# Two more buffers for rows of x in the last stage, loaded further ahead

## The chip, the cores and the metric

The kernel runs on one core of one Trainium2 chip. The metric is device time in microseconds (us). The kernel before took 1497.77 us (median of 3 runs, 1496.35 to 1498.45) when the work began.

Engine names in the profile: PE is TensorE's matmuls, PEld its weight loads, DVE VectorE, ACT ScalarE, POOL GpSimd, SP the engine that issues most loads. A "q" after a name (SPq) is that engine's instruction queue. "L1389" is line 1389 of the kernel.

## The reference, cut to what matters

The kernel computes the output of one block and its gradients. The block is a layer norm with modulation, a spectral filter, a second layer norm and a gated MLP. x has 2048 rows of 576 in bf16; the kernel holds them as 16 tiles of 128 x 576, each called "a row" below.

```python
h = _layernorm(x, axis=-1) * (1 + ca) + sa
x = x + ga * _A_ref(h, A_w_r, A_w_i)          # rfft2 * W, irfft2
h = _layernorm(x, axis=-1) * (1 + cb) + sb
x = x + gb * _B_ref(h, w_gate, w_up, w_down)  # the output, and B's gradients
_out, _vjp = jax.vjp(f, A_x, A_w_r, A_w_i, B_w_gate, B_w_up, B_w_down, c, w_mod)
```

The last stage of the kernel finishes the gradient of x: for each row it transforms back, normalises x again, applies the backward formula of the layer norm and stores the row. Two other jobs fill the stage: the rest of the output (`y_piece`, which keeps PE busy through `fill.run`) and the gradient of w_mod (`mod_grad`).

## The kernel before

The places of the buffers in SBUF, the loads, and the row loop (cuts are marked with `...`). `Ring(...).next()` hands out buffers in turn; a load into a reused buffer waits until the last reader of that buffer is done.

```python
with tc.manual_schedule(engines={PE}):       # only PE keeps the order of the text
...
x_r = Ring(span(RA, 3, 1152) + [ACC + 14464], [D])       # four buffers for x
gl_r = Ring(span(RA + 3456, 3, 1152) + [ACC + 15616], [D])
...
def load_xg(j):
    load1(xl, x_r, x_v, j, sp)                           # x row j, on SP's queue
    load1(gl, gl_r, gx1_d, j, sp)
...
for j in range(3):
    load_xg(j)
...
for j in range(18):
    if j < 16:
        if j and j + 2 < 16:
            load_xg(j + 2)
        Hs[j] = stage_bi(j, Gt, e_r, H_r)                # PE; L585 on ACT, L587/L588 on DVE
    ...
    if 1 <= j < 17:
        jj = j - 1
        stage_ai(Hs[jj])
        gh = gh_r.next()
        ac.copy(halves(gh), bank[:, 2:4, 0:288])         # L1387
        n = xl[jj]
        act(n[:], n[:], ACT.Identity, bias=..., scale=...)            # L1389, in place
        ...
        tt(gn[:], gh[:], opc, MUL)                                    # L1393
        tt(q[:], gh[:], n[:], MUL)                                    # L1394
        tt(t2[:], q[:], opc, MUL)                                     # L1395
        act(gn[:], gn[:], ACT.Copy, scale=..., accum_out=s[:, 0:1])   # L1396
        act(t2[:], t2[:], ACT.Copy, scale=..., accum_out=s[:, 1:2])   # L1397
        ts(s[:, 0:1], s[:, 0:1], -1.0 / D, None, MUL)                 # L1398
        act(t2[:], n[:], ACT.Identity, bias=..., scale=...)           # L1399, last reader of x
        tt(gn[:], gn[:], t2[:], ADD)                                  # L1400
        tt(gn[:], gn[:], gl[jj][:], ADD)                              # L1401
        ...
        fill.run(2.2)                                    # y's matmuls L1087, copy out L1090
    fill.run(2.2)
    ...
    while mdone < min(18, 6 * j // 5):
        ...
        mod_grad(*mgs[k], i)                             # L1259 (reads w_mod), L1260
        ...
```

## Time and profile before

The profiled run took 1495.91 us, its span 1494.1 us. The page's busy table and its chain of waits (what ended last, followed back to the start) say that TensorE is the limit of the whole:

```profile
PE 1458.8 (98%) x11108; PEld 968.2 (65%) x11108; DVE 773.3 (52%) x1651; ACT 549.5 (37%) x1048; POOL 347.8 (23%) x510
PE 80%; DMA 6%; DVE 5%; ACT 4%; issue 3%; POOL 1%; SPq 0%; DVEq 0%; ACTq 0%; POOLq 0%
```

So only what makes PE stand still, or slows its clock, in the last stage can cost time there. The PE timeline of the stage (start us, busy us, engine, line, operation; in brackets the idle time before it and what ended that) has four such places between 1376 and 1476 us:

```profile
1395.52 5.14 PE L1087 MATMUL bank<-arena 128*128 128x288 bf16 x27 [1.96 <-ACT arena L1090]
1420.00 0.40 PE L581 MATMUL bank<-arena 128*128 128x288 bf16 x2 [0.78 <-DVE arena L588]
1433.28 0.41 PE L581 MATMUL bank<-arena 128*128 128x288 bf16 x2 [1.23 <-DVE arena L588]
1441.91 3.47 PE L1087 MATMUL bank<-arena 128*128 128x288 bf16 x27 [0.59 <-ACT arena L1090]
```

The first is also followed by a slow spell: 27 matmuls take 5.14 us, against 3.47 us for the same 27 in the last line. The table of stretches shows the clock that was granted meanwhile (stretch, length, PE busy with its instructions, PE clock, DMA share, GB/s):

```profile
1395.00:1397.00 2.00, 1.48 (x12) 0.94 0.54 221
1397.00:1399.00 2.00, 2.00 (x10) 0.50 0.70 191
1399.00:1401.00 2.00, 2.00 (x14) 0.71 0.94 292
```

Why was ACT late? Its timeline just before the first stall:

```profile
1386.34 0.87 ACT L1399 ACTIVATE arena<-arena 128x576 bf16<-128x576 bf16 x1
1387.12 0.38 ACT L585 COPY arena<-bank 128x288 f32<-128x288 f32 x1
1387.40 0.64 ACT L1387 CAST arena<-bank 128x576 bf16<-128x576 f32 x1
1392.80 0.87 ACT L1389 ACTIVATE arena<-arena 128x576 bf16<-128x576 bf16 x1 [4.77 <-DMA arena<-in_A_x_dram]
1393.57 0.76 ACT L1396 ACTIVATE arena<-arena 128x576 bf16<-128x576 bf16 x1
```

And the same moment in the chain, in order of time:

```profile
1386.34 0.87 ACT arena L1399
1387.21 0.03 ACT arena L585
1387.24 5.54 DMA arena<-in_A_x_dram
1392.78 0.03 issue
1392.80 0.87 ACT arena L1389
```

Read these together. The L1399 at 1386.34 is row 0's, the L1387 at 1387.40 is row 1's, and L1396 at 1393.57 is row 1's. The L1389 at 1392.80 is row 4's: four L1389 had already run, the last from 1371.30 us. The load of row 4 could start only when row 0's L1399 had let go of the buffer, it took 5.54 us to land, and ACT stood still for it although row 4 was three rows away. The waits view sums such waits (engine, line, waited for: us in total, times, longest), for 1376 to 1494 us:

```profile
ACT arena L1389 <- DMA arena<-in_A_x_dram: 19.6, 9, 4.8
DVE arena L1259 <- DMA arena<-in_w_mod_dram: 7.6, 4, 2.5
```

The second line is on DVE: `mod_grad` stands in DVE's queue before its w_mod rows have landed, and L588, for which PE waits, stands behind it.

### The profile page before, as it was taken

Reading aid. Unit: us, or ns where it says so; the run is one execution under the profiler, and the core shown is the slowest. Engines: PE = TensorE matmul, PEld = TensorE weight load, DVE = VectorE, ACT = ScalarE, POOL = GpSimd, SP = SyncE. Lnnn points to the kernel's source line nnn. Section 1 sums busy time; section 2 is a strip of 40 time slices with the busy share of each in tenths; the row PEclk is TensorE's granted clock in tenths of the full one; section 3 lists DMA queues with packets and bytes.
Section 4 is the critical chain, followed back from the end, with each engine's and each line's share of the span. In section 5 each row is a group of like instructions: output and inputs, shape, how many; then the busy total and the mean of one; then the engine's idle time right before and its main releaser. Section 6 shows DMA issues by size and latency. Waiting matters only on the chain.

```text
span 1494.1 us, 28278 instructions
## 1 busy us (share of the span) xinstructions
PE 1458.8 (98%) x11108; PEld 968.2 (65%) x11108; DVE 773.3 (52%) x1651; ACT 549.5 (37%) x1048; POOL 347.8 (23%) x510
## 2 busy tenths in 40 slices
PE   8999999999999999999999999999999989999998
PEld 5444443677677677677677677677677666677666
DVE  6533596533543543543543543543543698577665
ACT  6756675212212212212212212212212266334566
POOL 1344322113113113113113113113112013242211
PEclk9999999999999999999999999999999999999999
DMA  9657996968477467568567467567567389667773
GB/s 347 176 150 158 225 242 165 215 132 174 122 130 178 120 128 178 119 130 178 120 129 177 119 130 178 120 130 177 119 124 161 78 225 302 231 212 195 232 240 101
DMA packets 417050, 252.79 MB, mean 169 GB/s; under 512 B 319730, under 2 KB 384692, under 8 KB 416660
## 3 DMA queue, kind: packets, MB, share of 16 engines
q1 hardware_dynamic: 388706, 166.53, 49.5%
q0 software_dynamic: 27440, 83.65, 18.4%
q8 instruction: 87, 1.43, 0.4%
q10 hardware_dynamic: 770, 0.80, 0.2%
q14 instruction: 47, 0.39, 0.1%
HBM read 98.52 MB, written 76.26 MB: 117 GB/s over the span
## 4 chain that ended last, share of the span: by engine, by line
PE 80%; DMA 6%; DVE 5%; ACT 4%; issue 3%; POOL 1%; SPq 0%; DVEq 0%; ACTq 0%; POOLq 0%
PE bank L807 9%; PE bank L809 8%; PE bank L838 8%; PE bank L885 8%; PE bank L889 8%; PE bank L944 5%; PE bank L1087 5%; PE bank L947 5%; PE bank L946 5%; PE bank L945 5%; PE bank L371 3%; PE bank L375 3%; PE bank L802 3%; PE bank L905 2%; DMA arena<-in_w_mod_dram 1%
## 5 line engine op out<-in xcount | busy, mean ns | idle before, releaser
L958 DVE TENSOR_TENSOR arena<-arena,bank 128x576 f32<-128x576 f32 x256 | 193.0, 754 | 307.1 <-PE bank L947 307.1
L813 ACT CAST arena<-bank 128x512 bf16<-128x512 f32 x144 | 84.4, 586 | 385.3 <-PE bank L803 377.0
L947 PE MATMUL bank<-arena 128*128 128x288 bf16 x576 | 164.9, 286 | 0.0
L944 PE MATMUL bank<-arena 128*128 128x288 bf16 x576 | 164.3, 285 | 0.4 <-DVE arena L956 0.2
L946 PE MATMUL bank<-arena 128*128 128x288 bf16 x576 | 164.7, 286 | 0.0
L945 PE MATMUL bank<-arena 128*128 128x288 bf16 x576 | 164.5, 286 | 0.0
L885 PE MATMUL bank<-arena 128*128 128x256 bf16 x1152 | 149.5, 273 | 3.6 <-DVE arena L871 1.8
L1087 PE MATMUL bank<-arena 128*128 128x288 bf16 x1152 | 150.0, 288 | 2.6 <-ACT arena L1090 2.6
L889 PE MATMUL bank<-arena 128*128 128x256 bf16 x1152 | 149.3, 273 | 0.0
L807 PE MATMUL bank<-arena 128*128 128x512 bf16 x576 | 148.7, 381 | 0.0
L809 PE MATMUL bank<-arena 128*128 128x512 bf16 x576 | 147.8, 379 | 0.0
L1087 PEld LDWEIGHTS <-arena 128*128 128x128 bf16 x1152 | 112.1, 98 | 34.7 <-issue 5.8
L838 PE MATMUL bank<-arena 128*128 128x288 bf16 x1024 | 128.1, 286 | 0.0
L885 PEld LDWEIGHTS <-arena 128*128 128x128 bf16 x1152 | 110.8, 98 | 20.6 <-issue 7.1
L889 PEld LDWEIGHTS <-arena 128*128 128x128 bf16 x1152 | 112.3, 98 | 13.7
L838 PEld LDWEIGHTS <-arena 128*128 128x128 bf16 x1024 | 100.2, 98 | 28.2
L817 DVE TENSOR_TENSOR arena<-arena 128x512 bf16<-128x512 bf16 x144 | 61.1, 424 | 105.6 <-ACT arena L813 101.6
L735 POOL DMA_DIRECT2D arena<-ghh_d x36 | 20.0, 556 | 395.2 <-DVE arena L816 386.8
L890 ACT CAST arena<-bank 128x256 bf16<-128x256 f32 x144 | 52.6, 373 | 140.8 <-PE bank L889 140.8
L807 PEld LDWEIGHTS <-arena 128*128 128x128 bf16 x576 | 50.4, 98 | 78.4 <-issue 31.2
L809 PEld LDWEIGHTS <-arena 128*128 128x128 bf16 x576 | 56.4, 98 | 67.9
L814 ACT CAST arena<-bank 128x512 bf16<-128x512 f32 x144 | 84.8, 589 | 22.4 <-PE bank L809 22.4
(269 smaller groups left out, 2313.2 us busy)
## 6 DMA issues: line engine op xcount, KB each, us to landing
ghh_d<-arena POOLq DMA_DIRECT2D x72, 256.0 KB, 3.9
arena<-ghh_d POOLq DMA_DIRECT2D x36, 512.0 KB, 5.9
hh_d<-arena SPq DMA_DIRECT2D x36, 512.0 KB
arena<-hh_d SPq DMA_DIRECT2D x32, 576.0 KB
out_dram<-arena POOLq DMA_DIRECT2D x67, 144.0 KB, 4.7
out_dram<-arena POOLq DMA_DIRECT2D x36, 256.0 KB, 5.1
arena<-in_B_w_down_dram POOLq DMA_DIRECT2D x18, 288.0 KB, 4.3
arena<-in_B_w_gate_dram POOLq DMA_DIRECT2D x18, 256.0 KB, 3.5
```

Source lines behind the costliest of these rows:

```text
L807: mm(bank[:, bg, :], w[:, m, fs], h2T[:, js, m, :], odd == 0 and m == 0, odd == 1 and m == 3)
L809: mm(bank[:, bu, :], w[:, 4 + k, fs], h2T[:, js, m, :], odd == 0 and k == 0, odd == 1 and k == 3)
L814: ac.copy(u[:], bank[:, bu, :])
L838: mm(bank[:, b0 + h, 0:288], sf[:, 0, fb, j, :], go[:, j, 288 * h:288 * h + 288], j == 0, j == 15)
L885: mm(bank[:, st["b"], 0:256], h2p[:, j, 128 * m:128 * m + 128], sf[:, 1 + w, :, j, :], j == 0, False)
L889: mm(bank[:, st["b"], 0:256], h2p[:, j, 128 * m:128 * m + 128], sf[:, 1 + w, :, j, :], False, j == 15)
L944: mm(o, xT[:, 1, 0, cs], wT[p][:, 0, 0, hs], True, False)
L945: mm(o, xT[:, 2, 0, cs], wT[p][:, 0, 1, hs], False, False)
L946: mm(o, xT[:, 1, 1, cs], wT[p][:, 1, 0, hs], False, False)
L947: mm(o, xT[:, 2, 1, cs], wT[p][:, 1, 1, hs], False, True)
L958: tt(dst, dst, src, ADD)
L1087: mm(bank[:, yb, 0:288], hl[:, fb % 18, 128 * (j % 2):128 * (j % 2) + 128], wdr[:, fb, 288 * h:288 * h + 288], fb == 0, fb == 35)
```

## The change

The intent: x comes late, so give it two more buffers, in space that a table of the stage before has left free, and load two rows further ahead.

```diff
-        x_r = Ring(span(RA, 3, 1152) + [ACC + 14464], [D])
+        x_r = Ring(span(RA, 3, 1152) + [ACC + 14464, ACC + 16768, ACC + 17920], [D])
...
         def load_xg(j):
-            load1(xl, x_r, x_v, j, sp)
+            while len(xl) < min(16, j + 3):
+                load1(xl, x_r, x_v, len(xl), sp)
             load1(gl, gl_r, gx1_d, j, sp)
```

(The extra line shifts later line numbers of the changed kernel by one: its L1390 is the old L1389, its L1400 the old L1399.)

## The prediction

> **What bounds the kernel now.** TensorE. The page's busy table gives PE 98% of 1494.1 us; the chain of waits is 80% PE, 6% DMA, 4% ACT. The change touches only the last stage (about 1376 us to the end). There the PE timeline has four idle spells: 1.96 us before 1395.5, 0.78 before 1420.0, 1.23 before 1433.3, 0.59 before 1441.9. From 1441.9 on the chain is PE alone, so nothing won there counts.
>
> **Which of it is x's.** The first and the last: PE waits for ACT L1090 (y's copy out of PSUM), and ACT sat idle before it until a load of x landed (4.77 us before L1389 at 1392.8, 1.91 us before L1389 at 1439.2). The other two are DVE L588 behind a w_mod load, which the change leaves. The first also cost clock: PE was granted 0.50 from about 1397 to 1400, and 27 matmuls took 5.14 us against 3.47 later, 1.67 us more. (The Trainium skill, "TensorE: Matmul & The Clock Gate", "What's actually happening", has half clock after an idle window of about 3.4 us; the trace agrees with the half clock, but 1.96 us of idleness was enough.) So all that x's loads cost is 1.96 + 1.67 + 0.59 = 4.2 us, 0.28%.
>
> **What the change removes, adds, moves.** No transfer or byte is added: 16 loads of 144 KB remain, issue about 0.33 us each. Two loads (rows 4 and 5) move from 1387 and 1396 into the stage before, into space that an inverse table leaves free.
>
> **Why I expect little of it.** Row 4 is loaded into row 0's buffer: its issue (1387.24) comes right after ACT L1399 of row 0 ends (1387.21), and it lands 5.5 us later. ACT has L1389 of row 4 in its queue ahead of L1396 of row 1: instructions have been sorted so that rows are normalised three ahead of their use (four L1389 had run before 1372). ACT stands still for a row that it doesn't need yet. ("PSUM — Partial Sum Buffer", "Engine vs sequencer instructions", says ScalarE's queue is strict FIFO; the trace agrees: L1396 follows with no gap, though its input was ready at about 1389.3.) After the change row j+4 goes into row j-2's buffer at the iteration at which row j+2 did, released by the same L1399. The time from release to issue is unchanged; only the row number is two higher. If the sorting again lets L1389 run as early as buffers allow, row 6 takes row 4's place and ACT waits as long at the same point.
>
> Gain comes only if the later L1389 are sorted behind the urgent work; then up to 4.2 us. Loss is possible if L1389 of rows 4 and 5 stall ACT before 1377 us (it already stood 4.94 us for x before 1371.3), delaying L572 or L585: 1 to 2 us.
>
> **Predicted.** 1497.2 us, 1494.0 to 1499.6 in 8 of 10. Faster by over 2%: 1%; within 2%: 98%; slower: 1%. About 65% no change within 1.5 us, 25% 2 to 4.5 us faster, 10% slower by 1 to 3.
>
> **What would show each step.** Right: six L1389 before row 0's L1396; the seventh right after L1399 of row 0, ACT idle about 5 us for in_A_x; PE idle about 2 us before a y matmul and half clock after it; ACT's total wait for x close to before's 28.1 us. Wrong: that wait under 10 us, and PE idle in the stage under 2.5 us.
>
> **What would make it wrong.** A different sorting of SP's or ACT's queue; the earlier loads colliding with loads of hh or the gate weights; the clock window catching another idle spell.

## The result

The changed kernel took 1497.11 us (median of 4 runs, 1496.11 to 1500.98) against 1497.84 us for the kernel before (4 runs). The ratio is 1.0001 with a 95% interval of 0.9981 to 1.0021: the same. Five more rounds later (run e11 below) gave 0.9999, interval 0.9983 to 1.0014.

The changed kernel's page, ACT timeline and waits view answer line for line to those shown above:

```profile
PE 1454.5 (97%) x11085; PEld 967.2 (65%) x11108; DVE 772.9 (52%) x1651; ACT 549.9 (37%) x1048; POOL 347.1 (23%) x510
1386.63 0.87 ACT L1400 ACTIVATE arena<-arena 128x576 bf16<-128x576 bf16 x1
1392.90 0.87 ACT L1390 ACTIVATE arena<-arena 128x576 bf16<-128x576 bf16 x1 [4.58 <-DMA arena<-in_A_x_dram]
1393.67 0.76 ACT L1397 ACTIVATE arena<-arena 128x576 bf16<-128x576 bf16 x1
ACT arena L1390 <- DMA arena<-in_A_x_dram: 18.6, 7, 4.6
DVE arena L1259 <- DMA arena<-in_w_mod_dram: 8.8, 4, 2.9
```

ACT stands still at the same point, 0.10 us later than before, for 4.58 us instead of 4.77. Six L1390 had run before it, so this one is row 6's. Over the whole span ACT waited 28.8 us for x, before 28.1. The PE timeline of the changed kernel, 1376 to 1476 us:

```profile
1395.62 3.47 PE L1087 MATMUL bank<-arena 128*128 128x288 bf16 x27 [1.84 <-ACT arena L1090]
1406.86 0.40 PE L581 MATMUL bank<-arena 128*128 128x288 bf16 x2 [1.11 <-DVE arena L588]
1413.23 0.41 PE L581 MATMUL bank<-arena 128*128 128x288 bf16 x2 [0.26 <-DVE arena L588]
1420.99 0.41 PE L581 MATMUL bank<-arena 128*128 128x288 bf16 x2 [1.66 <-DVE arena L588]
1434.82 0.41 PE L581 MATMUL bank<-arena 128*128 128x288 bf16 x2 [1.77 <-DVE arena L588]
1444.13 3.47 PE L1087 MATMUL bank<-arena 128*128 128x288 bf16 x27 [1.27 <-ACT arena L1090]
```

The stall before 1395.6 is there again. This run had no slow spell after it (27 matmuls in 3.47 us), and PE was idle more often later, 7.9 us in sum against 4.6 us. Behind L588 alone, which the prediction took as left unchanged, it was 4.8 us against 2.0; the second profile of the changed kernel (e11 below) has 4.5 us there, and why it rose was not traced. The stage had no gain to show.

The order in which the compiler put ACT's instructions tells why. To compare, the changed kernel was built with its new loop on one line, so that line numbers agree. PE's and POOL's order is the same in both kernels, DVE's differs in the order of four instructions, SP's in where the loads of x stand, and ACT's at three places only:

```
  L575                        L1389                       L585
+ L1389      (one earlier)    L1090                       L1387
  L488                      + L1389      (one earlier)  - L1389      (one fewer)
  L524                        L572 x4                     L1090, L1396, L1397, L1399, L585, L1387
  ...                         ...                       - L1389      (one fewer)
```

Two L1389 have come into the stage before, two have gone from the end of the row loop, and in between every instruction of ACT stands where it stood. Each L1389 in the loop now belongs to a row two higher.

### The profile page after: what moved, and what is told of

It reads as the page before. It is cut to its first block, busy times and chain, and to the rows that moved or that the text cites. A ratio compares the mean times of both kernels' runs of the same rounds, so it can differ in the third digit from the quotient of the medians.

```text
span 1496.3 us, 28254 instructions
## 1 busy us (share of the span) xinstructions
PE 1454.5 (97%) x11085; PEld 967.2 (65%) x11108; DVE 772.9 (52%) x1651; ACT 549.9 (37%) x1048; POOL 347.1 (23%) x510
## 4 chain that ended last, share of the span: by engine, by line
PE 83%; DVE 7%; DMA 4%; ACT 3%; issue 2%; SPq 0%; POOL 0%; DVEq 0%; ACTq 0%; POOLq 0%
PE bank L807 9%; PE bank L838 8%; PE bank L809 8%; PE bank L885 8%; PE bank L889 8%; PE bank L1087 5%; PE bank L944 5%; PE bank L947 5%; PE bank L946 5%; PE bank L945 5%; PE bank L371 3%; PE bank L375 3%; PE bank L802 3%; PE bank L905 2%; DMA arena<-in_w_mod_dram 2%
## 5 line engine op out<-in xcount | busy, mean ns | idle before, releaser
L1087 PE MATMUL bank<-arena 128*128 128x288 bf16 x1152 | 150.0, 288 | 3.1 <-ACT arena L1090 3.1
L1087 PEld LDWEIGHTS <-arena 128*128 128x128 bf16 x1152 | 112.1, 98 | 35.3 <-issue 6.2
L885 PEld LDWEIGHTS <-arena 128*128 128x128 bf16 x1152 | 110.8, 98 | 18.6 <-issue 5.2
```

The lines of the kernel that those rows point to most:

```text
L885: mm(bank[:, st["b"], 0:256], h2p[:, j, 128 * m:128 * m + 128], sf[:, 1 + w, :, j, :], j == 0, False)
L1087: mm(bank[:, yb, 0:288], hl[:, fb % 18, 128 * (j % 2):128 * (j % 2) + 128], wdr[:, fb, 288 * h:288 * h + 288], fb == 0, fb == 35)
```

## The experiments

Three theories about the mechanism. **Theory A**: ACT's queue runs in order, and the compiler puts each L1389 as early as the buffers allow; so ACT waits for a row that it doesn't need yet, and more buffers only raise that row's number. **Rival B**: x comes late because it has too few buffers or is loaded too late. **Rival C**: ACT's wait isn't what bounds the stage. After the first four runs theory A was extended to **A2**: there are two such eager consumers, L1389 on ACT and L1259 on DVE, and taking one away uncovers the other.

All variants gave correct results, and were timed in 5 rounds. The tool of most experiments is a tie: `tc.issue_after(i)` makes the compiler put an instruction behind `i` in the same engine's queue. It adds no semaphore, takes no wait away and moves no data. In all variants PE's order is unchanged. But the compiler sorts other instructions anew around a tie. With the tie on ACT only L1389 and three L1090 change places in ACT's queue, and some of DVE's instructions too. With the tie on DVE the loads of w_mod also change places in SP's queue (in e5 one is issued at 1395.68 us, ahead of the load of x at 1396.83; before, the load of x came first, at 1396.26, and w_mod's at 1397.77). So the tie on DVE is not a change of one place alone.

| run | x buffers | tie on ACT | tie on DVE | median us | ratio to before (95%) | PE busy of 1376 to 1476 us |
|---|---|---|---|---|---|---|
| before | 4 | no | no | | | 95.44 |
| changed | 6 | no | no | 1497.11 | 1.0001 (0.9981 to 1.0021) | 92.09 |
| e1 | 6 | no | no | 1497.28 | 1.0001 (0.9988 to 1.0013) | 94.43 |
| e2 | 4 | yes | no | 1495.7 | 0.9992 (0.9979 to 1.0005) | 93.85 |
| e3 | 6 | yes | no | 1494.78 | 0.9989 (0.9977 to 1.0002) | 93.73 |
| e4 | 15 | no | no | 1498.35 | 1.0012 (0.9999 to 1.0025) | 95.67 |
| e5 | 4 | no | yes | 1494.11 | 0.9987 (0.9971 to 1.0004) | 95.96 |
| e6 | 4 | yes | yes | 1487.28 | 0.9936 (0.9923 to 0.9950) | 100.00 |
| e7 | 6 | yes | yes | 1486.71 | 0.9933 (0.9920 to 0.9947) | 100.00 |
| e8 | 3 | yes | yes | 1492.54 | 0.9980 (0.9964 to 0.9995) | 98.28 |
| e9 | 6 | no | yes | 1495.55 | 0.9988 (0.9969 to 1.0006) | 95.79 |
| e10 | 15 | no | yes | 1490.68 | 0.9955 (0.9941 to 0.9969) | 99.95 |
| e11 (changed again) | 6 | no | no | 1497.93 | 0.9999 (0.9983 to 1.0014) | 93.96 |

The kernel before ran in the same rounds as each group: e1 to e4 1496.04 us (median of 11), e5 to e8 1495.89 us, e9 to e11 1497.08 us. The three groups ran on three different chips, so across groups only the ratios can be compared. PE busy doesn't show a clock spell, so the last column gives idle time alone.

### e1: the buffers alone

```diff
-        x_r = Ring(span(RA, 3, 1152) + [ACC + 14464], [D])
+        x_r = Ring(span(RA, 3, 1152) + [ACC + 14464, ACC + 16768, ACC + 17920], [D])
```

> Half of the change alone: six buffers for x, the load loop as before. The compiler sorts ACT's queue for this one differently from the changed kernel: most later L1389 stand behind the L1090 of the same row. Theory A (the place of L1389 in ACT's fixed queue decides): ACT's wait for x in the row loop falls from about 20 us to under 12 us and the 4.6 us stall after row 0's L1399 goes; time 1494 to 1497. Rival B (depth of buffers and distance of the loads decide): waits as in the changed kernel, about 28 us, since depth is the same; time 1497.

Measured: 1497.28 us (1493.54 to 1499.34), ratio 1.0001 (0.9988 to 1.0013). The expectation that the waits would fall was a miss: ACT waited 18.6 us for x in the stage, before 19.6. The compiler did sort ACT's queue in another way, and the long wait moved with it:

```profile
1401.47 0.87 ACT L1389 ACTIVATE arena<-arena 128x576 bf16<-128x576 bf16 x1 [5.73 <-DMA arena<-in_A_x_dram]
1402.24 0.76 ACT L1397 ACTIVATE arena<-arena 128x576 bf16<-128x576 bf16 x1
```

Here L1389 of a later row stands between L1396 and L1397 of a row in work. So it doesn't help that it stands behind that row's L1090: it still stands before something urgent. Unchanged waits and 1497 us are what rival B had said of this run, so it counts against A as it was put then; but with this other sorting L1389 is still early, so it can't decide between A and B.

### e2 and e3: the place of L1389, with four and with six buffers

```diff
-   act(n[:], n[:], ACT.Identity, ...)
+   with (tc.issue_after(sh[jj - 2].ins) if jj >= 2 else ExitStack()):
+       act(n[:], n[:], ACT.Identity, ...)
...
-   act(t2[:], n[:], ACT.Identity, bias=s[:, 0:1], scale=s[:, 1:2])
+   sh[jj] = act(t2[:], n[:], ACT.Identity, bias=s[:, 0:1], scale=s[:, 1:2])
```

e2 is the kernel before with this tie, e3 the changed kernel with it.

> The kernel before, four buffers and its loads unchanged; only L1389 of row j is tied behind L1399 of row j-2 in ACT's own queue (order alone, no semaphore). Theory A: ACT waits for x in the row loop fall from about 20 us to under 3 us with the old four buffers, the 1.96 us idle of PE before 1395 goes; time 1493 to 1496. Rival B: with four buffers x still lands late, waits stay above 10 us, time 1497 to 1498. Rival C (ACT's wait is not what bounds the stage): waits go, time stays at 1497 to 1498.

> The changed kernel with the same tie in ACT's queue. Theory A: same as the tie with four buffers within 1 us, so buffers five and six still buy nothing. Rival B: clearly better than with four buffers, by 2 us or more.

Measured: the waits for x in the stage are gone in both (no L1389 waits after 1376 us), with four buffers as with six. Rival B falls here: four buffers and loads no further ahead are enough for x to be in time. The medians lie in theory A's range (1493 to 1496 us), but the kernel before took 1496.04 us in these rounds. SP's order in e2 differs from before in one swapped pair of other loads, so the loads of x keep their places in the queue. But the time hardly moved, by 0.08% and 0.11%, both with 1 inside the interval. This is what rival C had said: the waits go, the time stays. The waits view and the PE timeline of e2 show what came instead:

```profile
DVE arena L1259 <- DMA arena<-in_w_mod_dram: 14.6, 4, 6.5
1405.85 0.41 PE L581 MATMUL bank<-arena 128*128 128x288 bf16 x2 [3.06 <-DVE arena L588]
1434.40 0.64 PE L581 MATMUL bank<-arena 128*128 128x288 bf16 x2 [2.70 <-DVE arena L588]
```

DVE's wait for w_mod rose from 7.6 to 14.6 us. With ACT in time, DVE reached L1259 sooner, but the load landed no earlier (L1259 began at 1401.52 us, before at 1401.96), so DVE's wait there grew from 2.46 to 6.48 us. PE lost 6.1 us idle in the loop (0.29 + 3.06 + 2.70), more than the 4.6 us before. After each of the two long stalls the clock fell to 0.50 as well, and 36 matmuls of L1087 took 5.96 and 6.87 us instead of 4.57, some 3.7 us more. (This profile is of the slowest of e2's five runs.) That led to theory A2.

### e4: fifteen buffers, no tie

```diff
-        x_r = Ring(span(RA, 3, 1152) + [ACC + 14464], [D])
+        x_r = Ring(span(RA, 3, 1152) + [ACC + 14464, ACC + 16768, ACC + 17920, ACC + 19072]
+                   + span(ACC + 24256, 6, 1152) + span(ACC + 31264, 2, 1152) + span(ACC + 33600, 2, 1152), [D])
...
-            load1(xl, x_r, x_v, j, sp)
+            while len(xl) < min(16, j + 12): load1(xl, x_r, x_v, len(xl), sp)
```

> Buffers for x from 4 to 15, loads as far ahead as they allow, no tie. The compiler then puts fifteen L1389 before row 0's L1396 and none into the row loop. Theory A: no wait for x in the row loop (under 2 us, before: about 20 us), but ACT waits 8 us or more for x before the loop, moved there rather than removed; time 1493 to 1498. Rival C: in-loop waits go and the time stays at 1497 to 1498 with PE idle elsewhere, at DVE L588 behind w_mod loads.

Measured: 1498.35 us, ratio 1.0012, so nothing gained; the time lies just above what both A and C had expected. ACT's wait for x in the stage fell to 0.8 us, but before the loop ACT waited 18.1 us for x. DVE waited 14.7 us for w_mod. The waits were moved, as A had said, and replaced, as C had said; PE's idle time in the loop (0.35 + 1.84 + 0.31 + 1.82) is all behind L588.

### e5: the place of the gate-weight work alone

```diff
-   tt(gn[:], gn[:], gl[jj][:], ADD)
+   og[jj] = tt(gn[:], gn[:], gl[jj][:], ADD)
...
-   mod_grad(*mgs[k], i)
+   with (tc.issue_after(og[j - 2].ins) if 2 <= j < 17 else ExitStack()):
+       mod_grad(*mgs[k], i)
```

> The kernel before (four buffers, ACT's queue free), only the gate-weight work L1259 of its loop place is tied behind L1401 of the row two before in DVE's queue. Theory A2 (two eager consumers, L1389 on ACT and L1259 on DVE, each hold their engine's fixed queue; taking one away uncovers the other): DVE's waits for w_mod fall from 5 us (12 to 15 us in the runs without x waits) to under 1 us, the ACT waits for x stay at 15 us or more in the loop, PE idle in the loop stays at 2 to 5 us, time within 1.5 us of before. Rival D (the gate weights alone were the limit): PE idle in the loop under 1 us, time 1493 or less.

Measured: 1494.11 us, ratio 0.9987 (0.9971 to 1.0004). No wait of L1259 for w_mod is left in the stage, and ACT still waits for x:

```profile
ACT arena L1389 <- DMA arena<-in_A_x_dram: 18.3, 11, 3.5
```

PE was idle 4.0 us in the loop. All this was as expected, but for the time: it lies 1.8 us under the kernel before, and 1.5 us was the limit given. Rival D (the gate weights alone) falls; one tie alone buys at most about 0.3% (the lower end of the interval) and perhaps nothing.

### e6 and e7: both ties, with four and with six buffers

e6 is the kernel before with the edits of e2 and e5, e7 the changed kernel with both.

> The kernel before with both ties, still four buffers. Theory A2: both waits gone, PE idle in the row loop under 1 us (before: 4.6, with either tie alone 2 to 6), no half-clock spell in the loop, time 1491 to 1494. Rival E (something third takes over, e.g. the loads gl or a slower chain because work is now later): PE idle stays above 2 us, time 1495 or more.

> The changed kernel with both ties. Theory A2: equal to the four-buffer kernel with both ties within 1 us; buffers five and six buy nothing even with the queues in order, since x then lands a row or more ahead already. Rival B: faster than four buffers by over 1.5 us.

Measured: 1487.28 us (1485.33 to 1488.81) and 1486.71 us (1484.83 to 1488.52), ratios 0.9936 and 0.9933, both intervals clear of 1. e6 was expected at 1491 to 1494 us, and came out 3.7 us under that range: the gain was underestimated. In both PE isn't idle once between 1376 and 1476 us, and no clock spell is left there. The table of stretches, before and then e6 (length, then busy us of PE, PEld, DVE, ACT, POOL with instructions, PE clock, DMA share, GB/s):

```profile
1376.00:1476.00 100.00, 95.44 (x753) 66.58 (x751) 67.54 (x190) 64.39 (x133) 22.09 (x38) 0.98 0.62 199
```

```profile
1376.00:1476.00 100.00, 100.00 (x809) 70.75 (x808) 72.54 (x202) 74.02 (x146) 23.69 (x41) 1.00 0.64 202
```

The same engines did more in the same 100 us, with the DMA share nearly unchanged. In ACT's timeline of e6 L1389 stands behind L1399 and costs only its own time:

```profile
1389.66 0.87 ACT L1399 ACTIVATE arena<-arena 128x576 bf16<-128x576 bf16 x1
1390.44 0.85 ACT L1389 ACTIVATE arena<-arena 128x576 bf16<-128x576 bf16 x1
1391.44 0.40 ACT L585 COPY arena<-bank 128x288 f32<-128x288 f32 x1 [0.16 <-PE bank L583]
```

Theory A2 holds and rival E (something third takes over) falls. ACT's order in e6 is that of e2, so these two differ only by the tie on DVE and what moved with it. Rival C was right about e2 and e3 only: with w_mod's wait out of the way, taking x's wait away does move the time (e5 to e6, 0.9987 to 0.9936). Either tie alone gave about 0.1%, both gave 0.64%. And six buffers against four: 1486.71 against 1487.28 us, with ranges that overlap almost wholly. Even with both queues in order, the change itself buys nothing that these runs can show.

### e8: both ties, three buffers

```diff
-        x_r = Ring(span(RA, 3, 1152) + [ACC + 14464], [D])
+        x_r = Ring(span(RA, 3, 1152), [D])
```

> Both ties, only three buffers for x: row j loads when row j-3 is done and is wanted one row later, 6 us after, against 2.4 to 5.5 us from issue to landing. Theory A2: at most some short waits of ACT for x (under 6 us in sum), time within 1.5 us of the four-buffer kernel. If depth does matter, waits above 10 us and 2 us or more slower.

Measured: 1492.54 us (1490.3 to 1496.96), some 5 us slower than e6, with 5.6 us of waits of ACT for x in the loop. The waits were within the expectation, the time was not: I had expected 1.5 us at most. PE's idle time in the stretch is only 1.7 us, with no slow spell, and the two profiled runs differ by 2.1 us (spans of 1488.5 and 1486.4 us), so what makes up the rest isn't shown. So depth does matter up to a point, and with the queues in order that point lies at four buffers, which the kernel already had.

### e9 and e10: six and fifteen buffers with the tie on DVE alone

e9 is the changed kernel, e10 the kernel of e4, each with the edit of e5.

> The changed kernel with the tie on DVE alone; ACT's queue is free, and is that of the same tie with four buffers but for two L1389 that have moved from its end to the stage before. Theory A2: depth buys nothing while L1389 is eager, even with the gate weights out of the way: ACT's waits for x in the loop 15 to 20 us (four buffers: 18.3), time 1493 to 1496, within 2 us of four buffers. Rival B: depth helps once the other limit is gone: waits under 10 us, time 1490 or less.

> Fifteen buffers and the tie on DVE. Every L1389 stands before the row loop, so no eager one is left in it. Theory A2: waits for x in the loop under 2 us and PE idle in the loop under 1 us, as with both ties; before the loop ACT still waits for x some 15 us, costing 0 to 2 us more than both ties: 1486 to 1490. If it stays at 1494 or more, the order of ACT in the loop is not the cause.

Measured: e9 took 1495.55 us, ratio 0.9988, like four buffers with the same tie (0.9987). ACT's queue in e9 is that of e5 but for two L1389 moved from its end to the stage before, and the waits stayed:

```profile
ACT arena L1389 <- DMA arena<-in_A_x_dram: 16.3, 7, 4.2
```

So w_mod's wait was not what hid a use of the two buffers. e10 took 1490.68 us, ratio 0.9955 (0.9941 to 0.9969): with fifteen buffers no L1389 is left in the loop, PE is busy 99.95 of the 100 us, and most of the gain is there without any tie on ACT. Before the loop ACT waited 19.4 us for x, which cost PE 1.01 us at one place (before 1364.4 us). By the ratios e10 is 0.2%, some 3 us, behind e6. Between their profiled runs it is 1.5 us (spans of 1487.9 and 1486.4 us), and 1.1 of these lie before the same L562 of PE (1370.69 and 1369.59 us), so ahead of the row loop; the rest was not traced. The expected range was 1486 to 1490, so this was just missed.

### e11: the changed kernel once more

> The changed kernel itself once more, for a narrower interval on another set of rounds. Theory A2 and the record: ratio to before 0.998 to 1.002.

Measured: 1497.93 us (1495.36 to 1498.92), ratio 0.9999 (0.9983 to 1.0014). ACT waited 17.8 us for x in the stage, and PE was idle 1.51 us at 1395.2 behind L1090, again without a slow spell after it. A slow spell came later in this run, after an idle time of PE behind L588, not behind L1090; the same 36 matmuls took 6.03 us, and 4.57 us the next time:

```profile
1434.13 0.41 PE L581 MATMUL bank<-arena 128*128 128x288 bf16 x2 [1.57 <-DVE arena L588]
1435.15 6.03 PE L1087 MATMUL bank<-arena 128*128 128x288 bf16 x36
1442.56 4.57 PE L1087 MATMUL bank<-arena 128*128 128x288 bf16 x36
```

## Why the prediction was right

**The time.** Predicted 1497.2 us (1494.0 to 1499.6), measured 1497.11 us: no change, as held for most likely. That it agrees to 0.1 us is luck: the runs of the changed kernel spread over 4.9 us, and in its profile two terms differ from the prediction and partly cancel, 1.67 us of slow clock that did not come and 2.8 us more of idle time behind L588.

**The mechanism.** "If the sorting again lets L1389 run as early as buffers allow, row 6 takes row 4's place and ACT waits as long at the same point." It does, to 0.10 us, with 4.58 us of waiting instead of 4.77, and the compiled order shows the shift by two directly. That this place in the queue, not depth, makes ACT wait is shown by e2: four buffers, loads where they stood, and no wait for x left in the loop. The Trainium skill, "PSUM — Partial Sum Buffer", "Engine vs sequencer instructions", calls ScalarE's queue strict FIFO; the trace of before agrees, for instance L1396 at 1393.57 us, at once after the L1389 that had waited.

**The possible loss.** It was said that L1389 of rows 4 and 5 might stall ACT before 1377 us. They did wait there (3.74 us before 1370.15 and 1.13 us before 1372.43 us), at no cost to PE.

**What was mis-sized.** "So all that x's loads cost is 1.96 + 1.67 + 0.59 = 4.2 us" and "then up to 4.2 us" took the idle spells behind ACT as the value of removing them. This step failed. Removing x's waits alone gave about 0.1% (e2, e3), since DVE's wait for w_mod grew from 7.6 to 14.6 us and PE stood behind that. Removing both gave more than both of before's terms together: 4.2 us of x and 2.0 us of w_mod make 6.2 us, and e6 gained about 9.6 us (0.64% of 1497). Between the two profiled runs alone the spans differ by 7.7 us (1494.1 and 1486.4): 6.2 us are those terms, and 0.7 us lie ahead of the row loop (the same L562 matmul of PE starts at 1370.28 and 1369.59 us). The rest is within the spread from run to run, and I haven't traced it further.

**The clock.** "Half clock after it" didn't appear in the changed kernel's first profile: PE idled 1.84 us, and 27 matmuls took 3.47 us. In its second (e11) there was a half clock, but after another stall. The Trainium skill, "TensorE: Matmul & The Clock Gate", "What's actually happening", says that the window of about 3.4 us runs freely; I infer that its place relative to a stall is chance. That agrees with the runs, where the length of a stall alone doesn't decide. For 27 matmuls: a slow spell after 1.96 us (before; 5.14 us) and after 3.19 us (e9; 6.25 us), none after 1.84 us (changed) and 1.51 us (e11; 3.47 us in both). For 36 matmuls, which take 4.57 us at full clock: a slow spell after 1.57 us (e11; 6.03 us) and 1.84 us (e4; 5.82 us), none after 2.31 us (e3; 4.57 us). I counted 1.67 us as a fixed part of the cost of x's wait; it is a part that some runs have.

## What to carry to other kernels

When an engine waits for a load, look at what it needs next, not only at what it waits for: if the data belong to a later step, the wait comes from the order of the queue, and a few more buffers let the eager instruction run ahead by just as much (here until all 16 rows were normalised before the loop, with 15 buffers in e10). Compare the compiled order before and after a change: here an order that had merely shifted went with waits and a time that stayed the same. And where several engines have such waits in one loop, remove them together before judging any of them, since each hides the other; here either tie gave about 0.1%, not clear of noise, and both gave 0.64%.

## What the Trainium skill lacked or had wrong

- "Perfetto Trace Analysis", "Optimization Strategy", says of repeated gaps that they "can mean there isn't enough SBUF/PSUM for the next tile to be allocated (buffer count, tile sizes)". It lacks the case shown here: the same gaps from an instruction sorted too early into an engine's queue. Two more buffers left ACT's waits in the stage at 18.6 us (before 19.6); a changed order with the old buffers left none.
- "TensorE: Matmul & The Clock Gate", "Why this matters for your kernels", advises no idle gap of PE over about 3 us. In the profiled run of before, 1.96 us of idleness were followed by a granted clock of 0.50 and 27 matmuls in 5.14 us instead of 3.47; and 1.57 us in e11 by 36 matmuls in 6.03 us instead of 4.57; gaps of 1.84 us (changed) and 2.31 us (e3) were not. So shorter gaps than the advice names can cost clock, in some runs.
- "DMA: Bandwidth & Descriptors", "Anatomy of one DMA — SWDGE (gpsimd) path", has a fit of 2.0 us plus bytes over 436e9, which makes 2.3 us for these 144 KB (an estimate from that page, and for another path: these loads are issued by SP). A load of x took 2.36 us at 1436.8 us, but 5.54 us at 1387.2 us, in a stretch where the DMA share was 0.97. The section has no figure for a load under such traffic (elsewhere the page has only an access latency at high load, not the time of a load), and it is the one that set the stall.
- No page says what an order of instructions chosen by the compiler does to a wait, or that ties on two engines are not additive: ratios 0.9992 and 0.9987 alone (both intervals include 1), 0.9936 together.
